# Eight experts with room by rank instead of equal room, the weights of experts 1 to 7 loaded from computed addresses

## The chip, the cores and the metric

One core of a Trainium2 chip runs the whole program. The metric is the device time of one execution in microseconds (us), as the median of several runs; lower is better. TensorE is called PE below (its weight loads PEld), VectorE DVE, ScalarE ACT, GpSimd POOL, and SyncE, which issues most transfers, SP.

## The reference

Three parts follow each other: attention over pooled keys, a layer of eight experts of which each token takes two, and a dense layer with a cosine. The part that matters here is the second one, with N = 4608 tokens, width 512, E = 8 experts and an inner width of 1024:

```python
noisy_logits = x @ w_gate + np.log1p(np.exp(x @ w_noise)) * noise
top2 = np.argpartition(-noisy_logits, 2, axis=1)[:, :2]
...
for e in range(E):
    for k in range(2):
        mask = top2[:, k] == e
        h = np.maximum(x[mask] @ w1[e], 0.0)
        out[mask] += top2_w[mask, k, None] * (h @ w2[e])
```

So 9216 rows (two for each token) are shared among eight experts, 1152 rows each on average. How many rows an expert gets depends on the data: for the inputs that the reference draws, its own router gives 1135, 1130, 1185, 1163, 1193, 1176, 1107 and 1127 rows for experts 0 to 7.

## The kernel before, in words

**Attention and routing (the first 290 us).** The attention output of 128 tokens at a time is split into two float16 parts and scattered by POOL (L565) into a table `xs` in device memory, in which expert e owns `ER` rows. A row's slot is its expert's start plus its rank among the rows of that expert. At the end, `ov1` to `ov3` (L694 to L725) count the rows of each expert and list blocks of 128 rows that go past the expert's room of `CAP` = 1216 rows. A loop (L746 to L781), which all engines enter and leave together, runs once for each such block; for counts of at most 1216 it runs not at all.

**The experts (about 300 to 1097 us).** Each expert's 1216 rows of room are cut into three chunks: 512, 512 and 192 rows (L783). A job is an expert and a chunk. `load_x` (L787) brings a chunk from `xs`, transposed, in one DMA that SP issues. `mm1` (L795) multiplies it with one 128-column block f of w1: 12 matmuls (4 blocks of the inner dimension, and three products of the float16 high and low parts) that move n columns, n being the rows of the chunk; then ACT (L819) and DVE (L820) write the two parts of relu(h) into `ht`. There are 8 such blocks in a job. `mm2` (L822) takes 128 rows of `ht` as the stationary side and moves the 512 columns of w2, in 24 matmuls; ACT scales the result (L835) and issues its DMA into the table `yb`.

**The last 64 rows of a chunk of 192.** They would need an `mm2` of their own with half of PE's columns idle. `mm2_pair` (L839) therefore takes the tails of two experts, e and e + 1, at once: 48 matmuls (L847), in turn one for expert e, whose result lies in PSUM rows 0 to 63, and one for expert e + 1, in rows 64 to 127. There are four pairs: (0, 1), (2, 3), (4, 5) and (6, 7). So that both tails are there at the same time, odd experts do chunk 2 first (L785).

**What sets the order.** All engines run the instructions in the order in which the program issues them. A list `work` holds the `mm1` and `mm2` steps; `mix` (L602) puts the `mm2` steps of a job among the `mm1` steps of the next. Next to each step hang small pieces of other work: the conversion of the next expert's weights (`prep_steps`, L117: load into `st`, maximum, scale, split into two float16 parts), the conversion of the third part's weights (L910), and `y_rows` (L859), which works out for each token the two rows of `yb` that the third part will gather. `load_x` for the next job is issued after the first `mm1` step of a job.

**The dense layer (1097 us to the end)** gathers rows of `yb` (POOL, L1036), adds them up, splits and transposes them (L1103, L1104) and multiplies.

Of the kernel before, what the change touches and what calls it, by code (L numbers as in the profile page):

```python
# [21 lines left out]
G, R = 4, 9  # L22
CAP = 1216
ER = CAP + 28 * 128
YS = E * CAP
# [9 lines left out]
def tile_attn_moe_ffn(ctx: ExitStack, tc: tile.TileContext, q, k, v, wgate, wnoise, noise,  # L35
# [152 lines left out]
    dl = const.tile([128, 8], F32, name="dl")  # L188
    PL.iota(dl, pattern=[[1024 - CAP, 8]], base=YS - CAP - 1024 * (E - 1), channel_multiplier=0, allow_small_or_imprecise_dtypes=True)
# [538 lines left out]
    for f in gt[:-1] + [scatter(G - 1, r_) for r_ in range(CUTS[4][1], R)] + [ov1, ov2, ov3] + gt[-1:]:  # L728
        f()
# [53 lines left out]
    CH = [(0, 512), (512, 512), (1024, CAP - 1024)]  # L783

    JOBS = [(e, c) for e in range(E) for c in ((0, 1, 2) if e % 2 == 0 else (2, 0, 1) if e < E - 1 else (0, 2, 1))]  # L785
    XT, HT, TAIL = {}, {}, {}

    def load_x(j):
        e, c = JOBS[j]
        o, n = CH[c]  # L790
        t = wp.tile([128, 8, 512], F16, name="xt", bufs=2)
        SP.dma_start_transpose(t[:, :, 0:n], xs[e * ER + o:e * ER + o + n, :])
        XT[j] = t

    def mm1(j, f):  # L795
        e, c = JOBS[j]
        n = CH[c][1]
# [12 lines left out]
        parts = [(ht, 0, n)]  # L810
        if c == 2 and e == E - 2:
            if f == 0:
                TAIL[e] = wp.tile([128, 2, 8, 64], F16, name="ty", bufs=4)
            parts = [(ht, 0, 128), (TAIL[e], 128, n)]
        elif c == 2:
            TAIL[e] = ht[:, :, :, 128:192]
        for t, c0, c1 in parts:
            t, p = t[:, :, f, 0:c1 - c0], ps[:, c0:c1]
            A.activation(t[:, 0], p, AF.Relu)  # L819
            V.scalar_tensor_tensor(t[:, 1], p, 0.0, t[:, 0], op0=OP.max, op1=OP.subtract)  # L820

    def mm2(j, t):  # L822
        e, c = JOBS[j]
        o, n = CH[c]
# [11 lines left out]
        r0 = E * o + n * e + 128 * t  # L836
        A.dma_start(yb[r0:r0 + m, :], yt[0:m])

    def mm2_pair(e):  # L839
# [4 lines left out]
        for f in range(8):  # L844
            for a_, b_ in ((0, 0), (0, 1), (1, 0)):
                for h in range(2):
                    PE.matmul(ps[64 * h:64 * h + 64], TAIL[e + h][:, a_, f, :], w[h][:, b_, f, :], start=(i == 0),  # L847
                              stop=(i == 23))
                i += 1
        yt = wp.tile([128, 512], F32, name="yt", bufs=2)  # L850
        for h in range(2):
            hs = slice(64 * h, 64 * h + 64)
            A.activation(yt[hs], ps[hs], AF.Copy, scale=W["y", e + h][hs])
        for h in range(2):
            r0 = E * 1024 + (CAP - 1024) * (e + h) + 128
            A.dma_start(yb[r0:r0 + 64, :], yt[64 * h:64 * h + 64])


    def y_rows():  # L859

        V.scalar_tensor_tensor(dl, nb[:, 0:8], 128.0, dl, op0=OP.mult, op1=OP.add)
        n = G * 2 * R
        of = wp.tile([128, 1024], F32, name="yg", bufs=4)[:, 0:8 * n].rearrange("p (n e) -> p n e", e=8)
        V.tensor_mul(of, ohs.rearrange("p g k r e -> p (g k r) e"), dl[:, None, :].to_broadcast([128, n, 8]))
        t = wp.tile([128, 512], F32, name="tm", bufs=2)
        d1, d2 = t[:, 0:n], t[:, n:2 * n]
        V.reduce_sum(d1, of, axis=AX.X)
        rf, ef = (t.rearrange("p g k r -> p (g k r)") for t in (rks, ecs))
        V.scalar_tensor_tensor(d1, rf, float(CAP), d1, op0=OP.is_ge, op1=OP.mult)
        V.tensor_add(d1, d1, rf)  # L870
        V.tensor_scalar(d2, ef, float(CAP - 1536), 512.0 * (E - 1), op0=OP.mult, op1=OP.add)
        V.scalar_tensor_tensor(d2, rf, 1024.0, d2, op0=OP.is_ge, op1=OP.mult)
        V.tensor_add(d1, d1, d2)
        V.tensor_scalar(d2, rf, 512.0, 512.0 * (E - 1), op0=OP.is_ge, op1=OP.mult)
        V.tensor_add(d1, d1, d2)
        V.scalar_tensor_tensor(yidx.rearrange("p g k r -> p (g k r)"), ef, 512.0, d1, op0=OP.mult, op1=OP.add)
# [299 lines left out]
    for fn, *a in work:  # L1176
        begin.append(begin[-1] + (12 * CH[JOBS[a[0]][1]][1] if fn is mm1 else 12288) / 2400.0)
# [14 lines left out]
    rest = [(begin[first[e]], begin[first[e]] + 11) for e in range(1, E - 1, 2)]  # L1192
# [29 lines left out]
    sched[work.index((mm2_pair, E - 2))].append(load_wout[0])  # L1222
# [173 lines left out]
```

## Time and profile before

| what | value |
|---|---|
| median of 3 runs (lowest, highest) | 1842.35 us (1841.18, 1845.97) |
| profiled execution, first to last instruction (span) | 1814.0 us |
| median less span: what lies around the instructions | 28.35 us |
| PE busy, share of the span | 1721.6 us, 95% |
| DVE, ACT, POOL busy | 59%, 51%, 23% |
| mean granted clock of PE | 0.975 |

The profiled execution's own time is told only as its span; the runs' times include what lies before the first and after the last instruction. A busy share is an average over the three parts of the kernel, which have different limits, so the views by stretch of time and the chain of waits say more than these shares.

### The profile page before, as it was taken

Reading aid. Unit: us, or ns where it says so; the run is one execution under the profiler, and the core shown is the slowest. Engines: PE = TensorE matmul, PEld = TensorE weight load, DVE = VectorE, ACT = ScalarE, POOL = GpSimd, SP = SyncE. Lnnn points to the kernel's source line nnn. Section 1 sums busy time; section 2 is a strip of 40 time slices with the busy share of each in tenths; the row PEclk is TensorE's granted clock in tenths of the full one; section 3 lists DMA queues with packets and bytes.
Section 4 is the critical chain, followed back from the end, with each engine's and each line's share of the span. In section 5 each row is a group of like instructions: output and inputs, shape, how many; then the busy total and the mean of one; then the engine's idle time right before and its main releaser. Section 6 shows DMA issues by size and latency. Waiting matters only on the chain.

```text
span 1814.0 us, 28287 instructions
## 1 busy us (share of the span) xinstructions
PE 1721.6 (95%) x11160; PEld 1017.4 (56%) x11160; DVE 1061.6 (59%) x2016; ACT 928.8 (51%) x1843; POOL 423.0 (23%) x457
## 2 busy tenths in 40 slices
PE   5977975999999999999999998999999999999999
PEld 3655652464445544464445545666666666666665
DVE  7787684644666484527674144666656566565633
ACT  4766851323233243323333235777777777767765
POOL 1225663000100000001110013524434243333222
PEclk8988986999999999999999999999999999999999
DMA  9978446456453738474744443313223031222100
GB/s 277 316 249 324 152 163 186 143 177 198 128 169 116 186 99 259 128 213 109 224 123 112 180 145 122 88 35 76 65 70 78 34 88 50 73 61 63 42 24 24
DMA packets 233206, 243.48 MB, mean 134 GB/s; under 512 B 154352, under 2 KB 167664, under 8 KB 232432
## 3 DMA queue, kind: packets, MB, share of 16 engines
q1 hardware_dynamic: 210544, 183.97, 35.0%
q0 software_dynamic: 11520, 37.76, 6.3%
q10 hardware_dynamic: 11008, 19.93, 3.1%
q8 instruction: 88, 1.44, 0.3%
q14 instruction: 46, 0.38, 0.1%
HBM read 127.06 MB, written 78.12 MB: 113 GB/s over the span
## 4 chain that ended last, share of the span: by engine, by line
PE 87%; DVE 8%; ACT 2%; issue 1%; DMA 1%; POOL 1%; SPq 0%; ACTq 0%; POOLq 0%; DVEq 0%
PE ph L1289 20%; PE ph L807 20%; PE py L832 19%; PE py L1252 15%; PE xp L450 3%; PE pt L1252 3%; PE sc L369 2%; DVE w L242 1%; PE py L847 1%; PE tr L416 1%; PE tr L353 1%; PE sc L254 1%; DVE amw L137 1%; DVE w L154 1%; ACT w L153 0%
## 5 line engine op out<-in xcount | busy, mean ns | idle before, releaser
L807 PE MATMUL ph<-xt,w 128*128 128x512 f16 (+1 forms) x2304 | 410.9, 336 | 11.1 <-DMA xt<-xs 11.1
L1289 PE MATMUL ph<-w,ht 128*128 128x512 f16 x1728 | 413.1, 379 | 1.0 <-POOL ht L1279 1.0
L832 PE MATMUL py<-w,ht 128*128 128x512 f16 x1728 | 384.4, 379 | 0.1
L807 PEld LDWEIGHTS <-w 128*128 128x128 f16 x2304 | 214.9, 98 | 198.0 <-issue 16.8
L1279 POOL TENSOR_TENSOR ht<-ty,ht 128x512 f16<-128x512 f32 x144 | 183.7, 1281 | 479.5 <-ACT ht L1278 323.8
L832 PEld LDWEIGHTS <-ht 128*128 128x128 f16 x1728 | 168.6, 98 | 199.1 <-DVE ht L820 0.6
L820 DVE SCALAR_TENSOR_TENSOR ht<-ph,ht 128x512 f16<-128x512 f32 (+2 forms) x192 | 109.9, 574 | 270.3 <-ACT ht L819 270.1
L1289 PEld LDWEIGHTS <-ht 128*128 128x128 f16 x1728 | 169.1, 98 | 152.8 <-POOL ht L1279 1.5
L1252 PEld LDWEIGHTS <-st 128*128 128x128 f16 x1872 | 183.1, 98 | 54.9 <-issue 4.0
L819 ACT ACTIVATE ht<-ph 128x512 f16<-128x512 f32 (+2 forms) x192 | 96.3, 502 | 184.4 <-PE ph L807 157.7
L835 ACT ACTIVATE yt<-py,ysc 128x512 f32<-128x512 f32 x72 | 49.4, 686 | 227.4 <-PE py L832 226.7
L1252 PE MATMUL py<-xt,st 128*128 128x256 f16 x1040 | 139.3, 273 | 3.5 <-ACT ht L1342 3.5
L1264 DVE SCALAR_TENSOR_TENSOR ty<-ty,k,ht 128x512 f32<-128x512 f32 x108 | 94.0, 871 | 83.1 <-ACT ty L1258 83.1
L1273 DVE SCALAR_TENSOR_TENSOR ty<-ty,ht 128x512 f32<-128x512 f32 x108 | 74.7, 692 | 108.8 <-ACT ty L1270 108.8
L1252 PEld LDWEIGHTS <-w 128*128 128x128 f16 x1152 | 112.7, 98 | 39.1 <-issue 3.8
L1269 ACT ACTIVATE ty<-ty,k 128x512 f32<-128x512 f32 x144 | 102.8, 714 | 22.9 <-DVE ty L1264 22.8
L1258 ACT ACTIVATE ty<-ht,k 128x512 f32<-128x512 f32 x108 | 77.4, 717 | 67.3 <-DVE ht L1343 34.1
L1252 PE MATMUL py<-w,st 128*128 128x256 f16 x832 | 111.7, 273 | 0.0
L1278 ACT ACTIVATE ht<-ty 128x512 f16<-128x512 f32 x144 | 89.5, 622 | 34.9 <-DVE ty L1273 34.3
L898 POOL TENSOR_TENSOR tm<-yg 128x512 f32<-128x512 f32 x32 | 33.8, 1057 | 302.7 <-DVE x L908 151.9
L1036 POOL DMA_INDIRECT yg<-yb,yidx x72 | 73.1, 1015 | 113.3 <-DMA yb<-yt 93.5
L1270 ACT ACTIVATE ty<-ty 128x512 f32<-128x512 f32 x144 | 90.7, 630 | 4.6
(249 smaller groups left out, 2095.2 us busy)
## 6 DMA issues: line engine op xcount, KB each, us to landing
yb<-yt ACTq DMA_DIRECT2D x72, 256.0 KB, 3.2
st<-in_moe_w_dram SPq DMA_DIRECT2D x8, 2048.0 KB, 13.5
yg<-in_moe_w_in_dram SPq DMA_DIRECT2D x32, 512.0 KB, 4.9
yg<-in_moe_w_out_dram SPq DMA_DIRECT2D x32, 512.0 KB, 4.4
yb<-zt SPq DMA_DIRECT2D x18, 768.0 KB, 19.8
st<-in_moe_w_dram SPq DMA_DIRECT2D x8, 1536.0 KB, 7.7
w<-in_k_dram SPq DMA_DIRECT2D x16, 512.0 KB, 5.8
w<-in_v_dram SPq DMA_DIRECT2D x16, 512.0 KB, 8.8
```

Of the source, the lines that this page charges most:

```text
L807: PE.matmul(ps[:, 0:n], w[:, a_, k_, 128 * f:128 * f + 128], xt[:, 4 * b_ + k_, 0:n], start=(i == 0), stop=(i == 11))
L819: A.activation(t[:, 0], p, AF.Relu)
L820: V.scalar_tensor_tensor(t[:, 1], p, 0.0, t[:, 0], op0=OP.max, op1=OP.subtract)
L832: PE.matmul(ps[0:m], ht[:, a_, f, 128 * t:128 * t + m], w[:, b_, f, :], start=(i == 0), stop=(i == 23))
L1252: PE.matmul(o, FW["in"][4 * a_ + 2 * sa + k_][:, f:f + 128], x[:, :, sb, k_, :], start=(start and h == 0 and k_ == 0 and j == 0), stop=(k_ ...
L1258: A.activation(y, h, AF.Identity, bias=CB["k4", c][:, 0:1])
L1264: V.scalar_tensor_tensor(y, y, CB["k4", c][:, 0:1], h, op0=OP.subtract, op1=OP.subtract)
L1269: A.activation(y, y, AF.Sin, scale=CB["k4", c][:, 1:2])
L1270: A.activation(y, y, AF.Square, scale=math.sqrt(2.0 * CC))
L1278: A.activation(g[:, 2 * b, :], y, AF.Copy)
L1279: PL.tensor_sub(g[:, 2 * b + 1, :], y, g[:, 2 * b, :])
L1289: PE.matmul(ps, g[:, 2 * b + a_, 256 * h + 128 * tt:256 * h + 128 * tt + 128], FW["out"][b_][:, k_, :], start=(q_ == 0 and b < 2 and h == ...
```

## The change

Room is no longer equal. Expert 0 has 1152 + 64 rows. Experts 1 to 7 are put in the order of their counts, largest first; the place in this order decides the room: 64, 64, 32, 32, 0, 0 and 0 rows over 1152 for places 1 to 7. Which expert stands at which place is known only at run time, so `ov1` works out each expert's place and room on DVE, a new step `order` makes a table `ids` of expert numbers and of first rows, and SP reads that table into registers before each load of x, w1 and w2 for places 1 to 7. Everything else in the stage (chunks, buffers, rows of `yb`) goes by place, with sizes fixed in the program. Chunk 2 now has 192, 192, 192, 160, 160, 128, 128 and 128 rows. Pairs are left for places (0, 1) and (2, 3) only; the pair of places 2 and 3 joins a tail of 64 rows with one of 32. Place 4's 32 rows get an `mm2` of their own, and places 4 to 7 do chunk 2 in the middle or at the end, without a pair. `y_rows` finds a row of `yb` through tables by expert.

```diff
+EXTRA = [64, 64, 64, 32, 32, 0, 0, 0]
+T0 = [E * 1024 + 128 * i + sum(EXTRA[:i]) for i in range(E)]
-YS = E * CAP
+YS = E * 1152 + sum(EXTRA)
...
         def load():
             X["t"] = ow.tile([128, 4096], F32, name="st", bufs=2)
             t = X["t"].rearrange("p (k f) -> p k f", k=kk)
+            if e > 0:
+                ee = nc.values_load(TE["ids"][0:1, 0, e:e + 1], engines=[mybir.EngineType.SP], min_val=0, max_val=E - 1)
+                if nm == "w2":
+                    SP.dma_start(t, src[bass.ds(ee, 1)].rearrange("e (k p) f -> p (e k) f", p=128))
+                    return
...
+    def order():
+        V.tensor_tensor(srt, pos_[:, None, :].to_broadcast([128, 8, 8]), num[:, :, None].to_broadcast([128, 8, 8]),
+                        op=OP.is_equal)
+        V.tensor_mul(srt, srt, num[:, None, :].to_broadcast([128, 8, 8]))
+        ef = ac.tile([128, 8], F32, name="ef")
+        V.reduce_sum(ef, srt, axis=AX.X)
+        V.tensor_copy(TE["ids"][:, 0, :], ef[0:1])
+        V.tensor_scalar(TE["ids"][:, 1, :], ef[0:1], float(ER), None, op0=OP.mult)
...
+        V.tensor_copy(cnt, p[:, 0:8])
+        key = ac.tile([128, 8], F32, name="key")
+        V.scalar_tensor_tensor(key, cnt, 16.0, tie, op0=OP.mult, op1=OP.add)
+        V.tensor_tensor(srt, key[:, None, :].to_broadcast([128, 8, 8]), key[:, :, None].to_broadcast([128, 8, 8]),
+                        op=OP.is_gt)
+        V.reduce_sum(pos_, srt, axis=AX.X)
...
-    for f in gt[:-1] + [scatter(G - 1, r_) for r_ in range(CUTS[4][1], R)] + [ov1, ov2, ov3] + gt[-1:]:
+    for f in gt[:-1] + [scatter(G - 1, r_) for r_ in range(CUTS[4][1], R)] + [ov1, ov2, ov3, order] + gt[-1:]:
...
-    CH = [(0, 512), (512, 512), (1024, CAP - 1024)]
+    def ch(e, c):
+        return (512 * c, 512 if c < 2 else 128 + EXTRA[e])
...
-    JOBS = [(e, c) for e in range(E) for c in ((0, 1, 2) if e % 2 == 0 else (2, 0, 1) if e < E - 1 else (0, 2, 1))]
+    JOBS = [(e, c) for e in range(E) for c in ((2, 0, 1) if e in (1, 3) else (0, 1, 2) if e < E - 1 else (0, 2, 1))]
...
+        row = nc.values_load(TE["ids"][0:1, 1, e:e + 1], engines=[mybir.EngineType.SP], min_val=0, max_val=(E - 1) * ER)
+        SP.dma_start_transpose(t[:, :, 0:n], xs[bass.ds(row + o, n), :])
...
-                    PE.matmul(ps[64 * h:64 * h + 64], TAIL[e + h][:, a_, f, :], w[h][:, b_, f, :], start=(i == 0),
+                    PE.matmul(ps[64 * h:64 * h + EXTRA[e + h]], TAIL[e + h][:, a_, f, :], w[h][:, b_, f, :], start=(i == 0),
...
+        def pick(d, tab):
+            V.tensor_mul(of, oh, tab[:, None, :].to_broadcast([128, n, 8]))
+            V.reduce_sum(d, of, axis=AX.X)
+
+        pick(d1, ta)
...
+        pick(d2, tb)
...
+        pick(d2, cap)
+        V.tensor_tensor(d2, rf, d2, op=OP.is_ge)
+        pick(d3, td)
...
-            dn = [(mm2, j - 1, t) for t in range(4 if c < 2 else 1)]
-            if c == 2 and e % 2 == 0 and e < E - 2:
+            dn = [(mm2, j - 1, t) for t in range(4 if c < 2 else 2 if e == 4 else 1)]
+            if c == 2 and e in (0, 2):
                 work += up + dn
                 continue
-            if c == 2 and e % 2:
+            if c == 2 and e in (1, 3):
                 work.append((mm2_pair, e - 1))
```

Three places show how instructions move. The first is PE at the pair of experts 2 and 3, after the last matmul of a normal `mm2`; `ht` is the stationary side and `w_...` the two experts' w2. Before:

```order
L832 MATMUL py<-w_5133,ht 128x512
L847 LDWEIGHTS ht
L847 MATMUL py<-w_5133,ht 64x512
L847 LDWEIGHTS ht
L847 MATMUL py<-w_5756,ht 64x512
```

and with the change (here `mm2_pair` is at L889):

```order
L874 MATMUL py<-w_5256,ht 128x512
L889 LDWEIGHTS ht
L889 MATMUL py<-w_5256,ht 64x512
L889 LDWEIGHTS ht
L889 MATMUL py<-w_5915,ht 32x512
```

The two matmuls of a step stand in turn, 24 times, as before; one of them now writes 32 rows where both wrote 64.

The second is DVE between the last ranks and the prefix sums of `ov2`. Before, two instructions stand there:

```order
L542 SCALAR_TENSOR_TENSOR idx<-ecs,rks 128x2
L701 TENSOR_SCALAR vb<-tr,thr 128x8
L702 TENSOR_TENSOR val<-val,tr 128x8
L707 COPY pre<-tr 128x8
L709 TENSOR_TENSOR pre<-pre 128x8 x2
```

With the change there are eleven:

```order
L732 COPY cnt<-tr 128x8
L734 SCALAR_TENSOR_TENSOR key<-cnt,tie 128x8
L735 TENSOR_TENSOR srt<-key 128x64
L737 TENSOR_REDUCE place<-srt 128x8
L738 TENSOR_SCALAR cap<-place 128x8
L739 TENSOR_SCALAR key<-place 128x8
L740 SCALAR_TENSOR_TENSOR cap<-cap,key 128x8
L741 TENSOR_SCALAR key<-cap,thr 128x8
L743 TENSOR_TENSOR vb<-cnt,key 128x8
L744 TENSOR_TENSOR val<-val,cnt 128x8
L745 TENSOR_TENSOR val<-val,cap 128x8
```

Eight of them come ahead of or make `vb`, which `ov2` needs, one after the other; five more of `order` stand between `ov3` and the loop.

The third is SP, where the loads of a later expert stand. Before:

```order
L792 DMA_TRANSPOSE xt<-xs 128x8x512
L129 DMA st<-in_moe_w_dram 128x3x1024
L131 DMA st<-in_moe_w_dram 64x1024 x2
L888 DMA yg<-in_moe_w_out_dram 128x1024 x6
L792 DMA_TRANSPOSE xt<-xs 128x8x192
```

With the change:

```order
L840 TENSOR_LOAD ids
L840 ISA x2
L841 ISA
L841 DMA_TRANSPOSE xt<-xs 128x8x512
L131 TENSOR_LOAD ids
L131 ISA x2
L135 ISA
L135 DMA st<-in_moe_w_dram 128x3x1024
L137 ISA
L137 DMA st<-in_moe_w_dram 64x1024
```

Each of the 21 loads of x and 14 loads of weights for places 1 to 7 now has a register load and register instructions ahead of it in SP's queue.

## Rows read from the trace of the kernel before

**Rows 1.** The page: busy time of PE; granted PE clock in 40 slices.
```profile
PE 1721.6 (95%) x11160; PEld 1017.4 (56%) x11160; DVE 1061.6 (59%) x2016; ACT 928.8 (51%) x1843; POOL 423.0 (23%) x457
...
PEclk8988986999999999999999999999999999999999
```
**Rows 2.** A stretch: length, busy us of PE, PEld, DVE, ACT, POOL; clock, DMA.
```profile
400.00:800.00 400.00, 400.00 (x2174) 201.65 (x2172) 222.66 (x368) 128.65 (x200) 17.26 (x17) 1.00 0.55 163
```
**Rows 3.** Chain of waits at the pair (0, 1): start us, us, what.
```profile
395.31 8.91 PE ph L807 x108
404.23 5.18 PE py L832 x24
409.40 5.30 PE py L847 x48
414.70 2.70 PE ph L807 x12
```
**Rows 4.** Timeline of PE at the pair (6, 7): start us, us, instruction.
```profile
1043.83 1.15 PE L807 MATMUL ph<-xt,w 128*128 128x192 f16 x12
1044.91 0.40 PE L847 MATMUL py<-w,ty 128*64 128x512 f16 x1
...
1045.15 0.38 PE L847 MATMUL py<-w,ty 128*64 128x512 f16 x1
...
1049.90 0.38 PE L847 MATMUL py<-w,ht 128*64 128x512 f16 x1
1050.21 2.76 PE L807 MATMUL ph<-xt,w 128*128 128x512 f16 x12
```
**Rows 5.** Timeline of PEld in the routing: weight loads for 8 matmuls.
```profile
232.41 0.40 PEld L522 LDWEIGHTS <-onesb 128*128 128x128 bf16 x8
232.74 0.10 PEld L525 LDWEIGHTS <-onesb 128*128 128x128 bf16 x1
```
**Rows 6.** Timelines of DVE, POOL, SP and PE from routing to experts.
```profile
284.13 0.37 DVE L709 TENSOR_TENSOR pre<-pre 128x8 f32<-128x8 f32 x2
...
290.08 0.96 POOL L565 DMA_INDIRECT xs<-xr,idx  x1 [0.21 <-issue]
...
291.71 0.16 DVE L556 TENSOR_TENSOR gates<-gates,g_w 128x1 f32<-128x1 f32 x1
...
295.35 8.31 SPq L792 DMA_TRANSPOSE xt<-xs  x2
...
301.51 16.00 PE L807 MATMUL ph<-xt,w 128*128 128x512 f16 x60 [11.12 <-DMA xt<-xs]
```
**Rows 7.** DMA issues: what, engine, count, median us from issue to landing.
```profile
xs<-xr,idx POOLq DMA_INDIRECT x72, 2.7
...
xt<-xs SPq DMA_TRANSPOSE x24, 6.4
```
**Rows 8.** Timelines of DVE and PE around `y_rows`.
```profile
332.42 0.76 DVE L864 TENSOR_TENSOR yg<-ohs,dl 128x576 f32<-128x576 bf16 x1
333.21 0.75 DVE L867 TENSOR_REDUCE tm<-yg 128x72 f32<-128x576 f32 x1
...
337.03 0.69 DVE L820 SCALAR_TENSOR_TENSOR ht<-ph,ht 128x512 f16<-128x512 f32 x1 [1.12 <-ACT ht L819]
...
339.62 0.69 DVE L820 SCALAR_TENSOR_TENSOR ht<-ph,ht 128x512 f16<-128x512 f32 x1 [0.77 <-ACT ht L819]
...
341.67 0.23 DVE L104 COPY mbc<-amw 128x128 f32<-128x128 f32 x1
...
346.56 0.27 PE L110 MATMUL pt<-idf,mbc 128*128 128x128 f32 x1
```
**Rows 9.** Waits of SP's queue: total us, times, longest.
```profile
SPq L956 <- DVE ty L955: 213.9, 37, 26.2
```
**Rows 10.** Timelines of SP and PE where the experts end.
```profile
1073.74 17.45 SPq L1104 DMA_TRANSPOSE xt<-x2h  x7
...
1097.39 1.47 PE L1252 MATMUL py<-xt,w 128*128 128x256 f16 x12
```

More of the change, by code (lines that the diff above doesn't have):

```diff
@@ L115, in tile_attn_moe_ffn @@
     WSRC = {"w1": (w1, 4), "w2": (w2, 8)}
+    TE = {}
     def prep_steps(e, nm):
@@ L125, in load @@
             t = X["t"].rearrange("p (k f) -> p k f", k=kk)
+            if e > 0:
[3 more added lines that the diff above has]
+                    return
+                SP.dma_start(t[:, 0:3, :], src[bass.ds(ee, 1), 0:384, :].rearrange("e (k p) f -> p (e k) f", p=128))
+                for h in range(2):
+                    SP.dma_start(t[64 * h:64 * h + 64, 3, :],
+                                 src[bass.ds(ee, 1), 448 - 64 * h:512 - 64 * h, :].rearrange("e p f -> p (e f)"))
+                return
             if nm == "w2":
@@ L187, in tile_attn_moe_ffn @@
     PL.iota(pp, pattern=[[0, 1]], base=0, channel_multiplier=1, allow_small_or_imprecise_dtypes=True)
-    dl = const.tile([128, 8], F32, name="dl")
-    PL.iota(dl, pattern=[[1024 - CAP, 8]], base=YS - CAP - 1024 * (E - 1), channel_multiplier=0, allow_small_or_imprecise_dtypes=True)
+    num = const.tile([128, 8], F32, name="num")
+    PL.iota(num, pattern=[[1, 8]], base=0, channel_multiplier=0, allow_small_or_imprecise_dtypes=True)
+    tie = ac.tile([128, 8], F32, name="tie")
+    PL.iota(tie, pattern=[[-1, 8]], base=0, channel_multiplier=0, allow_small_or_imprecise_dtypes=True)
+    V.memset(tie[:, 0:1], 1.0e6)
+    cnt = ac.tile([128, 8], F32, name="cnt")
+    srt = ac.tile([128, 8, 8], F32, name="srt")
+    pos_ = const.tile([128, 8], F32, name="place")
+    cap = const.tile([128, 8], F32, name="cap")
     wgn = ac.tile([64, 8, 16], F32, name="wgn")
@@ L691, in tile_attn_moe_ffn @@
     tabs = const.tile([1, 3, OVT], I32, name="tabs")
+    TE["ids"] = const.tile([1, 2, 8], I32, name="ids")
+    def order():
[6 more added lines that the diff above has]
+        V.tensor_scalar(TE["ids"][:, 1, :], ef[0:1], float(ER), None, op0=OP.mult)
     novi = const.tile([1, 1], I32, name="novi")
@@ L809, in mm1 @@
                 i += 1
[L810 to L820, printed above, removed]
+        if c == 2:
+            TAIL[e] = ht[:, :, :, 128:n]
+        t, p = ht[:, :, f, 0:n], ps[:, 0:n]
+        A.activation(t[:, 0], p, AF.Relu)
+        V.scalar_tensor_tensor(t[:, 1], p, 0.0, t[:, 0], op0=OP.max, op1=OP.subtract)
     def mm2(j, t):
         e, c = JOBS[j]
-        o, n = CH[c]
+        o, n = ch(e, c)
         m = min(128, n - 128 * t)
@@ L851, in mm2_pair, with small @@
         for h in range(2):
-            hs = slice(64 * h, 64 * h + 64)
+            hs = slice(64 * h, 64 * h + EXTRA[e + h])
             A.activation(yt[hs], ps[hs], AF.Copy, scale=W["y", e + h][hs])
         for h in range(2):
-            r0 = E * 1024 + (CAP - 1024) * (e + h) + 128
-            A.dma_start(yb[r0:r0 + 64, :], yt[64 * h:64 * h + 64])
+            r0, m = T0[e + h] + 128, EXTRA[e + h]
+            A.dma_start(yb[r0:r0 + m, :], yt[64 * h:64 * h + m])
     def y_rows():
-        V.scalar_tensor_tensor(dl, nb[:, 0:8], 128.0, dl, op0=OP.mult, op1=OP.add)
+        def small(nm):
+            return wp.tile([128, 8], F32, name="yr" + nm)
@@ new lines, in y_rows @@
+        ta, tb, td, te = (small(x) for x in "abde")
+        V.tensor_scalar(ta, pos_, 512.0, None, op0=OP.mult)
+        V.tensor_scalar(tb, pos_, 32.0, 96.0, op0=OP.mult, op1=OP.add)
+        V.scalar_tensor_tensor(tb, pos_, 64.0, tb, op0=OP.mult, op1=OP.min)
+        V.tensor_scalar(tb, tb, float(sum(EXTRA)), float(E * 1024 - 1024), op0=OP.min, op1=OP.add)
+        V.scalar_tensor_tensor(tb, pos_, 128.0, tb, op0=OP.mult, op1=OP.add)
+        V.tensor_scalar(td, nb[:, 0:8], 128.0, float(YS), op0=OP.mult, op1=OP.add)
@@ L867, in y_rows @@
-        V.reduce_sum(d1, of, axis=AX.X)
-        rf, ef = (t.rearrange("p g k r -> p (g k r)") for t in (rks, ecs))
-        V.scalar_tensor_tensor(d1, rf, float(CAP), d1, op0=OP.is_ge, op1=OP.mult)
+        d1, d2, d3 = t[:, 0:n], t[:, n:2 * n], t[:, 2 * n:3 * n]
+        rf = rks.rearrange("p g k r -> p (g k r)")
+        oh = ohs.rearrange("p g k r e -> p (g k r) e")
+        def pick(d, tab):
+            V.tensor_mul(of, oh, tab[:, None, :].to_broadcast([128, n, 8]))
+            V.reduce_sum(d, of, axis=AX.X)
@@ L876, in y_rows @@
-        V.scalar_tensor_tensor(yidx.rearrange("p g k r -> p (g k r)"), ef, 512.0, d1, op0=OP.mult, op1=OP.add)
+        pick(d2, cap)
+        V.tensor_tensor(d2, rf, d2, op=OP.is_ge)
+        pick(d3, td)
+        V.tensor_mul(d2, d2, d3)
+        V.tensor_add(yidx.rearrange("p g k r -> p (g k r)"), d1, d2)
     f64 = win.dtype != F32
@@ L1176, in tile_attn_moe_ffn @@
     for fn, *a in work:
-        begin.append(begin[-1] + (12 * CH[JOBS[a[0]][1]][1] if fn is mm1 else 12288) / 2400.0)
+        begin.append(begin[-1] + (12 * ch(*JOBS[a[0]])[1] if fn is mm1 else 12288) / 2400.0)
     def at(t, f):
@@ L1191, in tile_attn_moe_ffn @@
     b0, b1 = begin[first[0]] + 22, begin[first[E - 1]] - 32
-    rest = [(begin[first[e]], begin[first[e]] + 11) for e in range(1, E - 1, 2)]
+    rest = [(begin[first[e]], begin[first[e]] + 11) for e in (1, 3)]
     each = (b1 - b0 - 11 * len(rest)) / len(bg)
@@ L1221, in tile_attn_moe_ffn @@
         sched[first[E - 1] + 2 + 2 * i].append(load_win[i])
-    sched[work.index((mm2_pair, E - 2))].append(load_wout[0])
+    sched[work.index((mm2, JOBS.index((E - 2, 2)), 0))].append(load_wout[0])
     o = work.index((mm2, JOBS.index((E - 1, 0)), 3))
```

34 lines of the change are left out of this document (21 added, 13 removed).

## The prediction

> **What bounds the kernel now.** First the page: PE is busy 1721.6 us of the span, 95%, and its granted clock is high in every slice after the first eight [rows 1]. An average does not say which stretch is full, so next the stretch table: in 400 us of the experts' stage PE is busy all 400.00 us at a granted clock of 1.00, the upper of its two levels (2.4 GHz), while DVE has work for 222.66 and ACT for 128.65 us [rows 2]. The chain of waits agrees: at the pair (0, 1) it runs along PE alone, matmul group after matmul group, with no other engine between [rows 3]. So from the first matmul on a chunk to the last `mm2`, the end moves by what PE's instruction stream gains or loses, and other engines count only where they come too late. Third, the timelines at both edges of the stage, for such lateness. The chain gives the prices: a matmul of 192 columns takes 8.91/108 = 82.5 ns, one of 512 columns 5.18/24 = 215.8 ns [rows 3]. By the two, a column costs 133.3/320 = 0.4166 ns.
>
> The sum is made against the profiled span, 1814.0 us. The median of the runs, 1842.35, lies 28.35 us above it, which is time around the instructions; I leave that unchanged and add the sum to the median. A measurement of this kernel can tell some 0.3%, 5.5 us, from no change.
>
> **Narrower chunks: -10.2 us.** `mm1` of a chunk 2 has 8 blocks of 12, 96 matmuls. Two places go from 192 to 160 columns (32 x 0.4166 = 13.3 ns less, x 192 = 2.6 us), three to 128 (26.7 ns less, x 288 = 7.7 us). This needs weight loads that keep up with 55.8 ns a matmul. Weight loads of 128 columns went by eight in 0.33 us, 41 ns each [rows 5], so I take no floor. As an estimate, the other side of this is in the Trainium skill, "TensorE: Matmul & The Clock Gate", section Back-to-back issue gap: it gives about 81 ns a matmul at 128 columns with a weight load before each, which would leave this step hardly a gain. By the same sentence 512 columns would take 131 ns, and the trace has 215.8, so I trust it little; the row with the nearest shape is weighed as a rival below.
>
> **Two pairs gone: -10.8 us.** Before the pair (0, 1) the last `mm2` ends at 404.23 + 5.18 = 409.41; the pair takes 5.30 us, and the group after it takes 2.70 where 12 x 0.2158 = 2.59 were due: 5.40 us in all [rows 3]. Pairs (4, 5) and (6, 7) no longer exist, 2 x 5.40.
>
> **Place 4's own `mm2`: +5.4 us.** It moves 24 x 512 columns for 32 rows, 24 x 0.2158 = 5.18, and is a change of shape in and out, 0.11 + 0.10 (next step).
>
> **The pair of places 2 and 3: +10.3 us.** This is the large unknown. Today both halves have 64 stationary columns, so neighbours run side by side: 48 matmuls in 5.30 us, two in each 0.22 us [rows 3]. Now each matmul stands between two of another width, 64 and 32 in turn, and no row has that. Rows do have a change from 128 to 64 columns and back [rows 4]. In: twelve matmuls of 192 columns from 1043.83 should end at 1044.82, but the pair, reckoned back from its second matmul by 0.22 us, begins at 1044.93: 0.11 us lost. Out: the last matmul begins at 1049.90 and the next shape at 1050.21, 0.31 us for one that otherwise takes 0.2155: 0.10 lost. Neighbours did not overlap there: the old shape ran out before the new began. If that holds for 64 next to 32, 48 matmuls take 0.2155 + 0.11 = 0.325 us each, 15.6 to 15.7 us against 5.40. The bounds: nothing, if they still overlap (0), and 48 x 0.40 us, the recorded length of such a matmul alone [rows 4], 19.2 us (+13.8). I take +10.3, because the rows with a change of shape are the nearest. The Trainium skill, "TensorEngine Tiling (Array Packing)", section Key Properties, says that changing the tiling mode, unlike changing the tile within a mode, drains TensorE. The changes of rows 4 look like that; no run here shows 64 and 32 in turn.
>
> **From routing to experts: +0.3 us.** DVE gets eight more dependent operations ahead of `ov2`, at 0.20 us a step by the prefix sums (two in 0.37) [rows 6], some 1.6 us, and five of `order`, 1.0 us. Today DVE ends at 291.87, while the last scatter is issued at 290.08, takes 0.96 us and lands 2.7 us later [rows 6, 7], at 293.7; the first x load goes at 295.35, and PE waits 11.12 us for it [rows 6]. So DVE has 1.6 to 2 us of slack for 2.6, and the loop's entry, which all engines share, may move by the remainder. Bounds 0 (more slack than I read) and 2.7 (none).
>
> **`y_rows`: +0.2 us.** Each `pick` is a multiplication and a reduction, 332.42 to 333.21 and as long again, 1.58 us [rows 8]. Three more and small operations are 6.8 us on DVE. Behind them wait DVE's half of relu and the copy `mbc` at 341.67, done at 341.90; DVE stands idle 1.12 + 0.77 us in between, which absorbs 1.9. The copy ends near 346.8, and its reader on PE stands at 346.56. PE works from a queue of blocks before that, so 0.2; at most 2.1 if relu comes late once as well.
>
> **SP and the end: 0.** 35 register loads with their instructions stand ahead of 21 loads of x and 14 of weights. SP already waits 213.9 us for DVE, the longest time 26.2 [rows 9]; x loads go a whole job ahead and land in 6.4 us [rows 7]. Without that cover a late load of x stops PE for as long as it is late (priced below). At the end the last transposes for the dense layer are issued from 1073.74 for 17.45 us and land 2.7 us later (the scatter's landing, the nearest I have), 1093.9; PE wants them from 1097.39 [rows 10]. A stage shorter by 5 us could use up these 3.5 us, up to 2 us; but the steps ahead of the transposes move up with the stage, so 0.
>
> **Sum.** -10.2 - 10.8 + 5.4 + 10.3 + 0.3 + 0.2 = -4.8 us: 1837.5 us, -0.26%.
>
> **The rivals.**
>
> *Halves of 64 and 32 still overlap.* Their PSUM rows and columns are apart as before, and only the width differs. The pair keeps 5.40 us: -4.8 - 10.3 = -15.1, 1827.2 us. Against it: both changes of shape in rows 4 cost something. Chance 0.16.
>
> *In turn, without a gap.* 48 x 0.2155 = 10.35 us, +5.0 instead of +10.3: some 1832.4 us. Chance 0.06.
>
> *Narrow matmuls are paced by their weights.* Nothing in the trace of this stage is under 82.5 ns; if that is the floor of load and matmul together, the step of -10.2 falls away: 1847.7 us, +0.29%. For it: no row of the experts is faster. Against it: 41 ns a load in the routing [rows 5]. Chance 0.05. This is the case in which the Trainium skill's 81 ns (the page above) holds.
>
> *Loads with a computed address land late (the slower side).* Place: the first job after a short one. The load is issued after the first `mm1` step of the job before and is covered by 7 steps of it (7 x 12 x 82.5 ns = 6.9 us) and its `mm2` and pair (5.18 + 5.40), with the next step some 18 us, for place 1; other short jobs cover 26 to 28 us. Today 6.4 us are needed [rows 7]. It decides from 18 us on. At 30 us, PE would stand 12 us at place 1 and 2 to 4 us at each of the four others, +22: 1859 us. For it: no load of x from a register address is in the trace, and each expert's rows now start where a register says. Against it: the bytes and the queue are the same. Chance 0.06.
>
> *The room is too small.* If an expert's count is over the room of its place, the loop runs, for every engine. By the reference's counts places 1 and 2 take 1193 and 1185 rows (room 1216), 3 and 4 take 1176 and 1163 (room 1184), 5 to 7 take 1130, 1127 and 1107 (room 1152), and expert 0 has 1135: all fit. The kernel's router rounds otherwise and could move a row or two; the closest margin is 8 rows. A block would cost at least its two products, 20 to 30 us with loads that nothing covers: 1867 us. Chance 0.03.
>
> **How the numbers follow.** The forecast has 0.64; its own range is 1834.5 (pair +7.5, half way between in turn and drained) to 1841 (pair +13.8). About a third of it lies below 1836.8, the bound of faster: 0.21. With the two overlapping rivals (0.22) faster is 0.43. Slower, above 1847.9, are late loads, overflow and half of the pacing case: 0.11. The rest, 0.46, cannot be told from no change. The range goes from 1826, with most of the overlap case in it, to 1843; it leaves out the pacing, late and overflow cases (0.14) and the edges.
>
> **What would show it.** In the new trace: the group of 48 at L889 for places 2 and 3 (5.3, 10.4, 15.7 or 19 us); the spacing of `mm1` matmuls of 160 and 128 columns (69.2 and 55.8 ns, or 82.5); no pair after place 3; the entry of PE's first x wait; the reader of `mbc`; and PE's waits for `xt` in the experts' stage, which should stay at none. I am wrong if the pair's length is not near 15.7, or if PE shows idle time in that stage.

## The result and the profile after

The change made the kernel slower: 1857.66 us, the median of 7 runs, against 1842.35 before; ratio 1.0065 (95% interval 1.0039 to 1.0090). Forecast were 1837.5 us and a range up to 1843.0.

Chips differ: the kernel before takes 1843.5 and 1843.9 us on two of the chips used here and 1815.1 and 1815.0 us on two others, and the whole difference lies ahead of the first `mm1`. The profile of before (span 1814.0) is like those of the quicker kind, the medians of 1842 like those of the other. So the 28.35 us that the prediction took for time around the instructions are no such thing: an execution of the changed kernel with a span of 1853.2 us took 1855.2. Ratios below compare runs on one chip, and stages are compared within a kind. On the quicker kind the ratio is 1.0040 (1.0026 to 1.0055), 7 us.

The page of the changed kernel, and the stretch of [rows 2]:

```profile
PE 1728.8 (93%) x11088; PEld 1012.8 (55%) x11088; DVE 1066.3 (58%) x2038; ACT 922.7 (50%) x1832; POOL 422.4 (23%) x458
...
PEclk8988885899999999999998999999999999999999
```
```profile
400.00:800.00 400.00, 400.00 (x2093) 195.99 (x2092) 225.44 (x373) 127.55 (x196) 17.27 (x17) 1.00 0.53 157
```

In that stretch nothing has changed: PE is full at the upper clock. From the ninth of the 40 slices on one digit of the clock is new, an 8 in the 22nd, 973 to 1019 us. [Rows 1] have 9s there. The list of waits of PE says what it is (engine, line, waited for: us in total, times, longest):

```profile
PE pt L112 <- DVE mbc L106: 10.3, 3, 9.5
PE ph L855 <- DMA xt<-xs: 9.6, 1, 9.6
```

The second is [rows 6]'s wait for the first x. The first is a new one, and large. Its place on the timelines of PE and DVE, in the same kernel run again on a quick chip (after_again):

```profile
958.58 5.34 PE L874 MATMUL py<-w,ht 128*128 128x512 f16 x24
963.76 3.42 PE L855 MATMUL ph<-xt,w 128*128 128x512 f16 x24
976.70 0.47 PE L112 MATMUL pt<-idf,mbc 128*128 128x128 f32 x1 [9.52 <-DVE mbc L106]
976.97 8.06 PE L874 MATMUL py<-w,ht 128*128 128x512 f16 x24
984.87 1.50 PE L855 MATMUL ph<-xt,w 128*128 128x128 f16 x24
```
```profile
945.58 1.28 DVE L168 SCALAR_TENSOR_TENSOR w<-st,sw1s,w 128x1024 f16<-128x1024 f32 x1 [6.11 <-ACT w L167]
...
974.39 0.68 DVE L862 SCALAR_TENSOR_TENSOR ht<-ph,ht 128x512 f16<-128x512 f32 x1
974.99 1.21 DVE L151 TENSOR_REDUCE amw<-st 128x1 f32<-128x1024 f32 x1
976.23 0.16 DVE L154 TENSOR_REDUCE amw<-amw 128x1 f32<-128x4 f32 x1
976.42 0.23 DVE L106 COPY mbc<-amw 128x128 f32<-128x128 f32 x1
```

PE has done the last wide block of place 6's second job and the first 12 matmuls of 128 columns (963.76, the two together x24), and then stands until 976.70 for the transposition that finds the scale of place 7's w2. DVE is not idle in this time: it does the relu of that same wide block at 974.39, some 8 us after PE finished it, then the last maximum of w2 (L151), then `mbc`. The wait also costs clock: the next 24 matmuls take 984.87 - 976.97 = 7.90 us instead of 5.18. The granted clock is 0.50, the lower level (1.2 GHz), from 977 to 981 us and 1.00 again from 983; over these 20 us its mean is 0.74:

```profile
965.00:985.00 20.00, 10.48 (x48) 4.62 (x46) 10.70 (x21) 3.15 (x6) 0.00 (x0) 0.74 0.34 92
```

In all 9.5 + 2.7 = 12.2 us. The kernel before stands at the same point with almost nothing to spare (DVE and PE):

```profile
949.81 0.23 DVE L104 COPY mbc<-amw 128x128 f32<-128x128 f32 x1
...
973.34 0.23 DVE L820 SCALAR_TENSOR_TENSOR ty<-ph,ty 128x64 f16<-128x64 f32 x1 [0.29 <-ACT ty L819]
```
```profile
950.87 0.27 PE L110 MATMUL pt<-idf,mbc 128*128 128x128 f32 x1
...
958.75 3.74 PE L807 MATMUL ph<-xt,w 128*128 128x512 f16 x24
962.33 5.64 PE L832 MATMUL py<-w,ht 128*128 128x512 f16 x24
```

`mbc` was there 0.8 us before its reader. And DVE was late even then: the first narrow block of place 6 left PE at 962.33, its relu ended at 973.57, 11.2 us later, and PE had matmuls enough in hand.

Stage by stage on the quick kind (before; change): to the first x matmul 301.51; 301.20. Experts' stage, from there to the first matmul of the dense part, 795.9; 802.6. The rest 716.6; 715.9. The stage lost 6.7 us where 5.1 were to be gained. Of the 15.3 us by which the medians on the slower kind differ, the traces of before_again and of the change show 5.9 in the experts' stage, 2.1 at the end of the routing (below) and 1.3 behind the experts; the rest is not traced to a cause.

### The profile page after: what moved, and what is told of

The parts are those of the page before. It is cut to its first block, busy times and chain, and to the rows that moved or that the text cites. A ratio compares the mean times of both kernels' runs of the same rounds, so it can differ in the third digit from the quotient of the medians.

```text
span 1853.2 us, 28333 instructions
## 1 busy us (share of the span) xinstructions
PE 1728.8 (93%) x11088; PEld 1012.8 (55%) x11088; DVE 1066.3 (58%) x2038; ACT 922.7 (50%) x1832; POOL 422.4 (23%) x458
## 4 chain that ended last, share of the span: by engine, by line
PE 78%; DVE 2%; ACT 1%; DMA 0%; issue 0%; ACTq 0%; DVEq 0%; SPq 0%
PE py L874 20%; PE ph L855 20%; PE ph L1352 20%; PE py L1315 15%; PE pt L1315 2%; PE py L889 1%; DVE amw L151 0%; DMA xt<-xs 0%; DVE w L168 0%; DVE ty L1327 0%; PE pt L112 0%; ACT w L167 0%; DVE x L1114 0%; DVE ht L862 0%; ACT ht L1341 0%
## 5 line engine op out<-in xcount | busy, mean ns | idle before, releaser
L855 PE MATMUL ph<-xt,w 128*128 128x512 f16 (+3 forms) x2304 | 399.2, 331 | 9.6 <-DMA xt<-xs 9.6
L874 PE MATMUL py<-w,ht 128*128 128x512 f16 (+1 forms) x1752 | 391.8, 381 | 0.0
L855 PEld LDWEIGHTS <-w 128*128 128x128 f16 x2304 | 205.2, 98 | 196.4 <-issue 13.2
L874 PEld LDWEIGHTS <-ht 128*128 128x128 f16 (+1 forms) x1752 | 171.4, 98 | 202.1 <-issue 3.2
L862 DVE SCALAR_TENSOR_TENSOR ht<-ph,ht 128x512 f16<-128x512 f32 (+3 forms) x192 | 108.0, 565 | 273.0 <-ACT ht L861 265.9
L1352 PEld LDWEIGHTS <-ht 128*128 128x128 f16 x1728 | 169.3, 98 | 152.8 <-issue 1.1
L861 ACT ACTIVATE ht<-ph 128x512 f16<-128x512 f32 (+3 forms) x192 | 94.5, 496 | 183.3 <-PE ph L855 156.2
L1315 PEld LDWEIGHTS <-w 128*128 128x128 f16 x1152 | 113.0, 98 | 39.6 <-issue 4.3
```

The lines of the kernel that those rows point to most:

```text
L855: PE.matmul(ps[:, 0:n], w[:, a_, k_, 128 * f:128 * f + 128], xt[:, 4 * b_ + k_, 0:n], start=(i == 0), stop=(i == 11))
L874: PE.matmul(ps[0:m], ht[:, a_, f, 128 * t:128 * t + m], w[:, b_, f, :], start=(i == 0), stop=(i == 23))
L1315: PE.matmul(o, FW["in"][4 * a_ + 2 * sa + k_][:, f:f + 128], x[:, :, sb, k_, :], start=(start and h == 0 and k_ == 0 and j == 0), stop=(k_ ...
L1352: PE.matmul(ps, g[:, 2 * b + a_, 256 * h + 128 * tt:256 * h + 128 * tt + 128], FW["out"][b_][:, k_, :], start=(q_ == 0 and b < 2 and h == ...
```

## The experiments

The theory after the result (A): every price on PE was right, and DVE, with its background work (preparation of the next expert's weights, conversion of the third part's), comes 10 us late at place 6. Rivals: the change lengthens the part ahead of the experts (B); DVE's lag is only where two marks of the schedule meet (D), or lies in the work itself (E). A mark is the time, in us of PE's work from the first step of an expert, at which the program hangs a piece of background work.

The table has all runs; "stage" is the experts' stage, "wait" the longest wait in place 6 and its tile. The kernel before has stages of 795.9 and 795.3 us. The first 60 matmuls of a stage take 14.4 to 16.0 us in these traces, where 12.95 are due at the upper clock, so stages that differ by 1.5 us or less are not told apart.

| kernel | us (before) | ratio, 95% | first mm1 | stage | wait |
|---|---|---|---|---|---|
| change | 1857.7 (1842.4) | 1.0065, 1.0039 to 1.0090 | 334.1 | 801.2 | 9.5 mbc |
| before_again | 1844.6 (1843.5) | 1.0003, 0.9976 to 1.0030 | 328.9 | 795.3 | under 1 |
| a_scl_late | 1849.2 (1843.5) | 1.0008, 0.9980 to 1.0036 | 330.8 | 795.1 | 2.5 ht |
| a_pair_padded | 1841.6 (1843.5) | 0.9974, 0.9947 to 1.0001 | 330.7 | 790.7 | 9.5 mbc |
| a_both | 1834.3 (1843.5) | 0.9915, 0.9886 to 0.9944 | 332.0 | 783.1 | 2.5 ht |
| after_again | 1821.9 (1815.1) | 1.0040, 1.0026 to 1.0055 | 301.2 | 802.6 | 9.5 mbc |
| a_place5_tail_first | 1815.2 (1815.1) | 1.0000, 0.9990 to 1.0009 | 301.3 | 795.3 | 4.1 ht |
| a_conv_40us_earlier | 1820.4 (1815.1) | 1.0029, 1.0016 to 1.0042 | 302.3 | 796.9 | 2.3 mbc |
| a_best | 1803.3 (1815.1) | 0.9934, 0.9917 to 0.9950 | 299.7 | 785.0 | 4.1 ht |
| a_places_192_wide | 1866.5 (1843.9) | 1.0105, 1.0047 to 1.0163 | 343.9 | 806.6 | 4.9 mbc |
| a_place5_and_rest | 1854.0 (1843.9) | 1.0057, 1.0029 to 1.0086 | 340.6 | 802.5 | 4.6 ht |
| a_best3 | 1843.4 (1843.9) | 0.9993, 0.9968 to 1.0018 | 326.9 | 793.0 | 4.6 ht |
| a_light_conversions | 1813.5 (1815.0) | 0.9988, 0.9979 to 0.9998 | 302.1 | 791.4 | 2.3 mbc |
| a_best4 | 1800.1 (1815.0) | 0.9922, 0.9905 to 0.9938 | 299.6 | 779.4 | none over 1 |
| a_best5 | 1803.8 (1815.0) | 0.9933, 0.9916 to 0.9949 | 302.4 | 783.6 | 1.4 ht |

**before_again**: no edit.

> The kernel before, unchanged, to have its trace next to the time of the same execution. Theory A (the 28 us between the median of before and its profiled span lie in the attention and routing part, whose length varies from one execution to another): span near 1840 us, experts start near 325 to 330 us instead of 301.5, the experts' stage again near 796 us and the dense part near 717. Theory B (the change itself lengthens attention and routing by some 30 us): experts start near 301 again, span near 1814, and the time around the instructions is 28 us.

Span 1840.8, first `mm1` at 328.9, stage 795.3: theory A. The part ahead of the experts is as long in the kernel before, so B falls. What remains of it on this kind of chip stands at the end of the routing (DVE and SP, before_again and then the change):

```profile
321.32 0.16 DVE L556 TENSOR_TENSOR gates<-gates,g_w 128x1 f32<-128x1 f32 x1
...
322.46 8.75 SPq L792 DMA_TRANSPOSE xt<-xs  x2
```
```profile
326.68 0.16 DVE L577 TENSOR_TENSOR gates<-gates,g_w 128x1 f32<-128x1 f32 x1
...
327.81 8.46 SPq L838 DMA_TRANSPOSE xt<-xs  x2
```

In both the x load follows DVE's last operation by 1.0 us, where [rows 6] have 3.5: there the scatters' landing sets it, here DVE. From the last `ov1` matmul to the first `mm1` it is 16.7 us before and 18.7 with the change, all of DVE's added work, 2.1 us. On the quick kind it is 18.7 and 18.9. All kernels here with `order` in that place take 18.1 to 19.2.

**a_scl_late**:

```diff
-    POS = {..., "w2": [12, 50, 53, 56, 59, 65, 68, 71, 74, 77]}
+    POS = {..., "w2": [12, 50, 53, 56, 59, 71, 74, 77, 80, 83]}
...
-        at(begin[first[e]] + 80, ysc(e + 1))
+        at(begin[first[e]] + 86, ysc(e + 1))
```

> The change, with the scale of w2 and what follows it taken 6 us later in each expert (65 to 71, and 68..80 to 74..86). Theory A (DVE is a few us behind PE at the scale of place 7's w2, PE waits 9.7 us for mbc there and loses another 2.3 us at the lower clock): no wait of more than 1 us on mbc in the experts' stage, 12 us less than the change, 1846 us. Theory C (DVE has too much work in this stretch in any case): the wait comes back at the next reader, at most 4 us gained, 1854 us or more.

The wait for `mbc` is gone, but the stage falls by 6.1 of the 12.2 us only: the next reader, an `mm2`, waits 2.5 us for ACT's half of the last relu, and from 1005 to 1010 us, behind it, the granted clock is 0.66. Between the two theories.

```profile
PE py L874 <- ACT ht L861: 2.5, 1, 2.5
```

**a_pair_padded**:

```diff
-            TAIL[e] = ht[:, :, :, 128:n]
+            TAIL[e] = ht[:, :, :, 128:192]
+            if e == 3 and f == 0:
+                PL.memset(ht[:, :, :, 160:192], 0.0)
...
-                    PE.matmul(ps[64 * h:64 * h + EXTRA[e + h]], ...
+                    PE.matmul(ps[64 * h:64 * h + 64], ...
```

> The change, with the tail of place 3 filled up to 64 columns with zeros (one POOL memset), so that both halves of the pair of places 2 and 3 have 64 columns. If the difference in width alone ends the overlap: the pair's 48 matmuls take 5.3 us instead of 15.7, and the kernel gains 10.3 us, 1847.5 us. If the time of the pair came from elsewhere (two w2, late tails): the pair stays at 15.7 us, 1858 us. If the shorter stretch makes DVE later still, PE's wait at mbc grows by up to the same 10 us and the time stays at 1855 to 1858 with a pair of 5.3 us.

The pair of places 2 and 3 on the chain of waits, in the change and padded (start, us, what):

```profile
632.30 5.18 PE py L874 x24
637.48 15.68 PE py L889 x48
653.16 2.70 PE ph L855 x12
```
```profile
628.71 5.18 PE py L876 x24
633.89 5.30 PE py L891 x48
639.19 2.70 PE ph L855 x12
```

Width alone does it: 10.4 us, and the stage falls by 10.6. The wait at `mbc` stayed at 9.5. The kernel's time fell by more than expected, but on this kind of chip runs of one kernel lie up to 18 us apart.

**a_both**: the two edits.

> Both edits together. If both theories hold and the parts add up: 1857.7 - 12 - 10.3 = 1835 us, 7 us under the kernel before. If DVE becomes the bound of the experts' stage, PE waits reappear: 1842 to 1847 us.

The parts add up to within 1.4 us: 801.2 - 6.1 - 10.6 = 784.5 for the stage, and 783.1 are measured. The wait of 2.5 us for `ht` is there as in a_scl_late.

**after_again**: no edit.

> The change, unchanged, beside the others on one chip. Theory A: PE waits again near 9.7 us for mbc of place 7's w2, at the same matmul (the order of the work makes it), the stage lasts 801 us, and the last ov1 matmul to the first x matmul takes 18.1 to 19.1 us against 16.7 in the kernel before; 1852 to 1858 us. If that wait was an accident of one execution it is gone: stage 789 us, 1845 us.

The wait is the same to a hundredth of a us (9.52), on another chip: the program's order makes it.

**a_place5_tail_first**:

```diff
-    JOBS = [... ((2, 0, 1) if e in (1, 3) else ...
+    JOBS = [... ((2, 0, 1) if e in (1, 3, 5) else ...
```

> The change, but place 5 does its chunk 2 first, as the odd experts did in the kernel before; nothing else. By the PE times that the schedule counts, the job after place 5 then has four mm2 steps between its mm1 steps instead of one, and the marks at 59 us (last maximum of w2) and 65 us (its scale) of place 6 fall on two wide mm1 steps with an mm2 between them, 8 us apart, instead of on a wide one and on the first narrow one, 0.6 us apart. Theory D (the new order of jobs moves the marks onto the narrow steps): no wait above 1 us on mbc in place 6, stage 789 us, 12 us less than the change. Theory E (DVE has fallen behind in place 6 whatever the grid, by the conversions): the wait stays above 5 us, at mbc or at ht.

The wait for `mbc` vanishes, as D has it, but PE then waits 4.1 us for `ht`, as E has it (PE):

```profile
966.45 4.70 PE L874 MATMUL py<-w,ht 128*128 128x512 f16 x21
975.29 1.51 PE L874 MATMUL py<-w,ht 128*128 128x512 f16 x3 [4.14 <-ACT ht L861]
```

**a_conv_40us_earlier**:

```diff
-    b0, b1 = begin[first[0]] + 22, begin[first[E - 1]] - 32
+    b0, b1 = begin[first[0]] + 22, begin[first[E - 1]] - 72
```

> The change, with the conversion of the third part's weights ending 72 instead of 32 us before place 7, so a little denser before and gone from the last 40 us of place 6. Theory E (DVE is behind there because conversion and preparation meet): no wait above 1 us in place 6, stage 789 to 790 us. Theory D alone (marks 0.6 us apart): the wait for mbc shrinks to the 2 to 4 us that the maximum and its copy take by themselves, stage 792 to 794 us. If the denser conversions put DVE behind elsewhere, a wait appears before place 6.

Place 6 keeps a wait of 2.3 us, where D had 2 to 4 and E under 1, and four more of 0.5 to 1.8 us appear ahead of it: conversions packed closer make DVE late elsewhere.

**a_best**: a_pair_padded and a_place5_tail_first, and

```diff
-    ... [ov1, ov2, ov3, order] + gt[-1:]
+    ... [ov1, ov2, ov3] + gt[-1:]
...
     load_x(0)
+    order()
```

> Place 5's tail first, the pair padded to 64 columns, and the step order moved behind the loop and the first x load (DVE does it while PE works). If all parts hold: stage 778 to 779 us, 1.0 us less from the last ov1 matmul to the first x matmul, dense part 717: with an attention part of 312 us a span of 1826 and about 1828 us, 15 us under the kernel before. If a new wait appears in the shorter stage, as ht did before: 1834 us.

From the last `ov1` matmul to the first `mm1` it is 18.0 us, 1.0 less than in after_again; but kernels with `order` ahead of the loop lie between 18.1 and 19.2, so this gain is not told from their spread. The wait for `ht` stays, and the stage is 785.0. A new limit shows behind it: the dense part takes 720.1 us. The chain there:

```profile
1079.94 4.98 PE py L877 x23
1085.66 11.44 DMA yb<-yt
...
1109.56 1.18 POOL ht L1346
1110.79 1.89 PE ph L1356 x4
```

The last rows of `yb` land 11.4 us after they are issued, the gathers follow, and PE waits 5.5 us for POOL.

**a_places_192_wide**:

```diff
-        return (512 * c, 512 if c < 2 else 128 + EXTRA[e])
+        return (512 * c, 512 if c < 2 else 192)
...
```

> The change, but chunk 2 moves 192 columns again at every place (only the rows within the room are used further on, so the output is the same); rooms, pairs, order and computed addresses stay. By the prices of the forecast it costs 10.2 us of PE time where PE is busy. Theory F (the narrow steps alone bring the wait for mbc): the wait is under 2 us, the stage 802 us: as long as the change's, since 10.2 us more work take the place of the 12 us. Theory D (the order of the jobs brings it, the width only adds 0.3 us a step): the wait stays at 8 to 9.7 us and the stage is 811 to 812 us, so that the kernel is 9 to 10 us over the change.

Neither F nor D: the wait is halved, to 4.9 us, and the stage is 806.6. So the narrower steps bring about half of the wait, and the new order leaves the rest (PE):

```profile
1019.36 0.48 PE L112 MATMUL pt<-idf,mbc 128*128 128x128 f32 x1 [4.87 <-DVE mbc L106]
```

**a_place5_and_rest**: a_place5_tail_first, and `rest` for places 1, 3 and 5.

> Place 5's tail first, and the 11 us without background pieces at the start of place 5 given back, so that marks and background pieces in places 5 and 6 lie nearly as in the kernel before; chunk widths, pairs and rooms as in the change. If the position of these pieces is all that makes PE wait: no wait over 1 us in the stage, 789 us, and 6 to 7 us less than the kernel before. If DVE's lag of some 11 us at the end of place 6's second job (11.3 us in the kernel before too) is now uncovered because the steps behind it are shorter, a wait of 2 to 5 us for ht stays: stage 792 to 796 us.

A miss: to put the pieces back where they were makes it worse, for the same pieces then stand closer (33 us of the stage are kept free of them instead of 22), and ahead of place 6 there are three more waits, of 2.3, 0.4 and 2.0 us.

**a_best3**: the same with the padded pair and the later `order`.

> The same with the padded pair and the step order behind the first x load. If there is no wait: stage 778 to 779 us. The dense part starts with the landing of the last rows of yb and the gathers (a_best: 720 instead of 716 us), so with 282 us up to ov1 and 18 us to the first x matmul a span of 1798 us and about 1799 us, 16 us under the kernel before; with a wait for ht left as in a_best, 1803 us.

The same waits; no gain.

**a_light_conversions**:

```diff
-                    to_f32(t, vv, X.pop(("mk", c)))
+                    if c < 8:
+                        to_f32(t, vv, X.pop(("mk", c)))
+                    else:
+                        V.tensor_copy(vv, X.pop(("mk", c)))
```

> The change, but of the last 8 conversions of the third part's output weights the three DVE operations that put the number's bits together are left out and replaced by one copy (so those weights, and the output, are other ones); some 2 us of DVE work less in each, about 15 us in places 5 and 6. Theory E (DVE's background work, which no part of the change reduced, puts it some 10 us behind PE where conversions and the preparation of place 7 meet, and the shorter matmul stream no longer hides that): PE's wait for mbc of place 7's w2 falls from 9.7 to under 2 us and the stage to 789 to 791 us. Theory D alone (only the two marks 0.6 us apart): the wait stays above 5 us, stage 796 us or more.

In each of the last 8 conversions one copy stands for four operations of DVE, so the output is another one. With marks, jobs and widths all as in the change, less DVE work alone takes the wait from 9.5 to 2.3 us and the stage to 791.4. So most of the wait goes with DVE's work, as E has it; the 2.3 that stay, just over the 2 expected, agree with D's 2 to 4 us that the maximum and its copy need by themselves (PE):

```profile
969.20 0.33 PE L112 MATMUL pt<-idf,mbc 128*128 128x128 f32 x1 [2.32 <-DVE mbc L106]
```

**a_best4** and **a_best5**: the padded pair and the later `order`; a_best4 also with place 5's tail first; and w2's marks (the load, four maxima, the scale, four splits):

```diff
+    POS = {..., "w2": [12, 50, 53, 56, 59, 71, 80, 83, 86, 89]}
```
```diff
+    POS = {..., "w2": [12, 50, 56, 67, 70, 76, 80, 83, 86, 89]}
```

> Padded pair, place 5's tail first, order behind the first x load, and w2's scale at 71 and its splits at 80 to 89 us of each expert, so that in place 6 they fall behind the second job. Theory E: the splits no longer stand ahead of the second job's last relus, the wait for ht (4.5 us with place 5's tail first) falls under 2 us, stage 779 to 781 us, 12 us less than the kernel before in all (part of the gain is lost where the gathers begin). If another reader takes the wait over: stage 785 us as in a_best.

> Padded pair, order behind the first x load, the change's own order of jobs, and w2's last two maxima at 67 and 70, its scale at 76 and its splits at 80 to 89 us, all behind the second job of place 6. Theory E: wait for ht (2.5 us with only the scale moved) falls under 1 us, stage 778 to 780 us; the kernel 12 to 14 us under the kernel before. If the lag is the conversions' alone, the wait for ht stays at 2 to 3 us, stage 782 to 783 us.

In a_best4 the wait of place 6 is gone (all of PE's waits of the stage behind the first x):

```profile
PE ph L856 <- DVE ht L865: 1.2, 2, 0.9
...
PE pt L112 <- DVE mbc L106: 0.4, 1, 0.4
```

It beats both kernels: 1800.1 us against 1815.0, ratio 0.9922. a_best5, with the change's own order of jobs, keeps a wait of 1.4 us for `ht`, where under 1 was expected, and its stage is 4.2 us longer; 1.5 of these are the clock of its first 60 matmuls (15.96 us against 14.44).

## Why the prediction was wrong

**Narrower chunks, -10.2: right.** Blocks of 128 columns (the change, PE):

```profile
1016.39 1.50 PE L855 MATMUL ph<-xt,w 128*128 128x128 f16 x24
1017.73 5.34 PE L874 MATMUL py<-w,ht 128*128 128x512 f16 x24
```

24 matmuls in 1.34 us, 55.8 ns each; 34 of 160 columns on the chain take 2.35 us, 69.1 ns. The rival of the pace of weight loads falls. With it falls, for this stream of 24 in a row, the 81 ns that the Trainium skill gives ("TensorE: Matmul & The Clock Gate", section Back-to-back issue gap): the trace disagrees, at 55.8.

**Pairs gone and place 4's own `mm2`: right.** Two pairs are left, and place 4's 24 matmuls of 32 rows take 5.29 us (849.45 to 854.74 us) with their changes of shape, against 5.4.

**The pair of 64 and 32 rows, +10.3: right,** at 15.68 us where 15.6 to 15.7 were worked out from [rows 4]. The rivals "overlap" and "in turn without a gap" fall. That a change of the tiling mode drains TensorE (the Trainium skill, "TensorEngine Tiling (Array Packing)", section Key Properties) agrees with these rows: the halves overlap again when padded to one width.

**From routing to experts, +0.3: right for the chip kind of the profile, too small for the other.** The slack of 1.6 to 2 us of [rows 6] is the scatters' lateness on one kind of chip; on the other there is none, and the term is 2.1, near the upper bound.

**`y_rows`, +0.2: right** (no wait at its place). **SP and late x loads: right**; no wait for `xt` but the first. The rival of the room that is too small falls too: the trace of the change has no matmul of the loop (L816). **The end, 0: right for this change,** but a_best shows the next limit there, and it is not the 3.5 us of the transposes: it is the last rows of `yb`, which POOL gathers.

**Where it failed** is the first part: "other engines count only where they come too late", followed by a look "at both edges of the stage" only. The bounds of the sum hold no term for the middle: DVE was looked at where the change adds work to it (`y_rows`), not where it takes matmuls away in front of DVE's readers. That stage was read from a stretch of 400 us in which DVE has 222.66 us of work, 56% [rows 2]. The stretch ends 150 us ahead of the wait; from 878 to 978 us, the 100 us of place 6, DVE is busy for 69.58 us in the kernel before. The sum of the terms of the stage (all but the +0.3) was -5.1 us; without the 12.2 us the stage is 802.6 - 12.2 = 790.4 against 795.9, -5.5. So the mechanism forecast is there to within 0.4 us, less than two stages can be told apart by, and one missing term turned its sign. The prediction's own sign of being wrong, idle time of PE in that stage and the reader of `mbc`, names it.

What the missing term is, step by step. Pieces of background work hang at marks in us of PE's work after the first step of an expert, and a mark becomes the first step that begins no earlier. Place 5 now ends with its narrow chunk, so place 6's first job has one `mm2` among its 8 wide steps (8 x 2.56 + 5.12 = 25.6 us by the schedule's own count) instead of four. Its second job then ends at 66.6. The last maximum of w2 (mark 59) falls on the step at 64.0, its scale (mark 65) on the next, the first narrow one at 66.6 us, with nothing but 12 narrow matmuls of 0.67 us between. Before, an `mm2` of 5.18 us and 12 wide matmuls of 2.59 us stood between them. DVE, late by some 8 us there, has nothing behind which to be late. In numbers, from PE's end of the block that the last maximum hangs on: before, `mbc` is done after 6.9 us (943.10 to 950.04), and PE has 7.8 us of matmuls; with the change it is done after 10.3 us (966.35 to 976.65), and PE has 0.7. So some 7 of the 10 us are matmuls that no longer stand between the two marks, and some 3 are a later DVE; a lag of 7 us was there before. Four runs show the parts: moving the marks apart, by the marks or by the order of jobs, removes the wait for `mbc`, but 2.5 to 4.1 us come back at `ht`; widening the steps halves it; taking DVE's work away takes three quarters of it.

Why DVE is late is seen on its timeline in part: a split of w1 that hangs on an `mm2` step lets it stand 6.1 us until ACT, which first evicts that `mm2`, has done its half, and each conversion passes from DVE to ACT and back. In the kernel before the same mark falls on an `mm1` step, and DVE waits 1.2 us there. How much of the lag each of these makes was not taken apart.

## What to carry to other kernels

When a change shortens the stream of the engine that bounds a stage, the background work of the others stays as long. Before counting the gain, list at each hand-over in the stage (here `mbc` and `ht`) how long before its reader the operand is ready. A margin of 0.8 us stood in the profile of before, at one row, and no average shows it. PE's list of waits does name the hand-over in the kernel before, with waits of 0.4 and 0.2 us at the first and the last expert:

```profile
PE pt L110 <- DVE mbc L104: 0.6, 2, 0.4
```

So there was nothing to spare. Work that is hung at marks of time moves when step lengths change, so the margins have to be read again on the new grid, in the order of the changed program. And two halves of PE that are to overlap can be worth filling up to one width: here it brought 10.4 us.

## What was not expected of the hardware

Two halves of PE with stationary tiles of 64 and 32 columns in turn cost 327 ns a matmul (15.68/48), against 110 when both have 64 (5.30/48): 32 columns less made the pair three times as long. This was forecast from rows of another change of shape, and no row had shown it. What was not forecast: the same program takes 28 us more on some chips, all of it ahead of the experts: there the first x matmul stands at 328.9 instead of 301.5 us in the kernel before. Engines show waits there that no semaphore of the program explains ("issue" and "remote" in the list of waits, 15.3 us for ACT's `xr` in before_again). What causes them was not tried.
